# Moving VectorE's multiplications by g and its row scalings to other gaps of a fused attention and gated-FFN kernel

## The chip, the core and the metric

The kernel runs on one core of a Trainium2 chip. The metric is the device time of one execution in microseconds (us), as the median of several executions. The engines are named as in the profile: PE multiplies matrices (PEld is its weight load), DVE is the vector engine, ACT the scalar engine, POOL the general-purpose engine, SP the engine that only issues transfers here. Each engine runs its own instructions in the order in which the program lists them; engines wait for each other through semaphores.

## What is computed

Linear attention without a softmax, a normalisation of each head's row, and a gated feed-forward layer:

```python
kv  = einsum('bhsd,bhse->bhde', k, v)        # 8 batches, 8 heads, 576 tokens, head size 64
o   = einsum('bhsd,bhde->bhse', q, kv)
x   = o / sqrt(mean(o*o, -1) + 1e-6) * g_norm  # then (tokens 4608, columns 512)
ffn = (gelu(x @ w_gate) * (x @ w_val)) @ w_out
out = x + sigmoid(x @ w_res) * ffn
```

Inputs and outputs are float32; the kernel multiplies in float16 with float32 sums.

## The kernel before, in words

**Blocks.** The work is cut into nine blocks of 512 tokens: blocks 0 to 7 are the first 512 tokens of each batch, block 8 collects the 64 left over from each. The attention of a batch is computed one or two blocks ahead, in gaps of the feed-forward work. Per block a tile `t` (128 partitions x 4 rows x 512 columns, float16) holds x, a transposing DMA makes `xT` of it, and `th_all` and `res_all` (the `osb` of the profile) hold the gate and the result. `res_all` and `th_all` exist once.

**Making x.** `a_t` (L330, its instruction on L341) scales one quarter of the attention's result by the rows' inverse norms: it reads the product in PSUM (`op`) and the norms in SBUF (`ny`) and writes `t`. Its numbers 0 to 3 are the four quarters and 4 the left-over rows. `a_x` (L353, instruction on L355) multiplies one row of `t` by `g16`, the vector g, in place: both inputs and the output are float16 in SBUF. For block 1 the transposed copy gets its g elsewhere, and the four `a_x` of block 1 are for the residual sum alone. They are the lambdas `x` at L570.

**The gate and value products.** From block 2 on, the products with `w_gate` (suffix g) and `w_val` (suffix v) are made in groups of four column tiles by `gv_group` (L708), with seven half-size products instead of eight. A group follows a list of words written out by hand (`ORDERS`, L703). `1g` to `7g` and `1v` to `7v` are products of four matmuls each on PE (L737); `Eg`, `Ev` copy `A` to another PSUM bank and `dg`, `dv` copy `F` to SBUF, on ACT (L747, L751); `Fg`, `Fv`, `cg`, `cv` are additions on DVE (L758); `g11` and so on are gelus on ACT (L768); `h11`, `h12`, `h21` are multiplications on DVE and `h22` one on POOL (L774). The order of a group that is not its block's last:

```
1g 1v Eg 5g Ev 5v dg 6g dv 6v Fg 2g Fv 2v 7g g11 7v cg 3g cv 3v h11 g12 4g g21 h12 4v g22 h21 h22
```

Products 1, 6, 7 and 4 of a letter share the bank `A` of that letter, so 6 waits for the copy E, 7 waits until the addition F has read `A`, and 4 until the addition c has. The next group takes the banks in another order: its `E` is this group's `F`, its `F` this group's `E`. So its copy `Ev` waits for this group's `h12`, the last reader of that bank.

**Work in the gaps.** `at_word(blk, i, word, fs...)` (L1172) hangs further instructions behind a word of group i of block blk. They stand in the order of each engine at that place, so that a DVE instruction hung on `1v` comes ahead of `Fg` on DVE, one hung on `Fv` between `Fv` and `cg`, one hung on `cv` between `cv` and `h11`.

**The end of a block.** `out_by_products` (L497) makes the last product and the gate; `fin` (L529, instruction on L531) adds `t` to a half of `res_all` on POOL, and `store` (L533, issue on L536) sends two rows to HBM from SP's queue. For block 1 the flag `later` is set, and `fin`, `store` and block 1's `a_x` are hung on words of the first group of block 2 (L569 to L574). Block 2 has its first columns in another form and then two groups; blocks 3 to 6 (`whole`, L1175) have three groups each. `plan_attn_ahead` (L1179) hangs the scalings `a_t` of batch b in block b-1 (its m+1): numbers 0 and 1 at the end of the block before it, numbers 2 and 3 in group 0 and number 4 in group 1 (L1220 to L1233).

The two places that the change touches and what calls them:

Of the kernel before, what the change touches and what calls it, by code (L numbers as in the profile page):

```python
# [18 lines left out]
def kernel(  # L19
# [392 lines left out]
    def m_res(blk, j, bank):  # L412
        rps = pmoe.tile([P, C], FP32, name="rps", bank=bank)
        for cc in range(NP):
            nc.tensor.matmul(  # L415
                rps,
                lhsT=xT_t[blk][:, j, cc, :],
                rhs=wr16[:, cc, :],
                start=(cc == 0),
                stop=(cc == NP - 1),  # L420
            )

        th = th_all[:, j, :]
        nc.scalar.activation(out=th, in_=rps, func=AF.Tanh, scale=0.5)  # L424
        return th
# [33 lines left out]
    def a_of(blk, i, j):  # L459
        return hids[blk][:, (j - 1) * NFH : j * NFH, (i - 1) * PR : i * PR]  # L460
# [20 lines left out]
    def s_last(blk):  # L481
        sub(nc.vector, hid_sums[3], a_of(blk, 1, 2), hid_sums[1])

    def prod(ps, a, b, start, es=(0, 1)):

        for e in es:
            for f in range(NFH):
                nc.tensor.matmul(  # L488
                    ps[:, e - es[0], :],
                    lhsT=a[:, f, e * P : (e + 1) * P],  # L490
                    rhs=b[:, f, :],
                    start=(start and e == es[0] and f == 0),
                    stop=(f == NFH - 1),
                    skip_group_check=True,
                )

    def out_by_products(blk, later, banks, amid):  # L497
        w = {}
        s_ = hid_sums

        def aside(ahead_of):
            for f in amid.get(ahead_of, ()):
                f()

        def res(jj):
            for j in (2 * jj, 2 * jj + 1):
                m_res(blk, j, banks[j])

        def first_two():
            for n in ("D", "E", "F", "A"):  # L510
                w[n] = pmoe.tile([P, 2, CH], FP32, name="w" + n, bank=banks[n])
            w["d"] = attnp.tile([P, 2, CH], FP32, tag="sq", bufs=3, name="wd")
            s_last(blk)
            prod(w["A"], a_of(blk, 1, 1), b_of(1, 1), True)
            nc.scalar.copy(out=w["E"], in_=w["A"])
            aside("D")
            prod(w["D"], s_[0], wo_t[:, 0], True)
            nc.scalar.copy(out=w["d"], in_=w["D"])
            aside("gates")
            for j in range(NJ):  # L520
                m_sigmoid(j)

        def part(jj):
            return slice(None), slice(2 * jj[0], 2 * jj[0] + 2), slice(jj[1] * CH, (jj[1] + 1) * CH)

        def pf(jj, src, eng=nc.vector):
            eng.tensor_tensor(out=res_all[part(jj)], in0=th_all[part(jj)], in1=src, op=ALU.mult)  # L527

        def fin(jj):  # L529
            of = part(jj)  # L530
            nc.gpsimd.tensor_tensor(out=res_all[of], in0=res_all[of], in1=t_t[blk][of], op=ALU.add)  # L531

        def store(jj):  # L533
            dst = out[blk * S : blk * S + M0, :].rearrange("(p j) c -> p j c", j=NJ)
            js = slice(2 * jj, 2 * jj + 2)
            nc.sync.dma_start(out=dst[:, js, :], in_=res_all[:, js, :])  # L536

        def others():


            prod(w["A"], s_[1], wo_t[:, 1], False)
            aside("F")
            sub(nc.vector, w["F"], w["A"], w["d"], ALU.add)
            aside("00")
            prod(w["E"], a_of(blk, 1, 2), b_of(2, 1), False)
            pf((0, 0), w["E"])
            aside("22")
            prod(w["A"], s_[2], wo_t[:, 2], False)
            c22 = res_all[part((1, 1))]
            sub(nc.vector, c22, w["A"], w["d"], ALU.add)  # L550
            aside("01")
            prod(w["F"], s_[3], b_of(2, 2), False)
            pf((0, 1), w["F"])
            aside("11")
            prod(w["A"], a_of(blk, 2, 2), wo_t[:, 3], False)
            if whole(blk + 1):
                pf((1, 1), c22, nc.gpsimd)
                pf((1, 0), w["A"])
            else:
                pf((1, 1), c22)  # L560
                pf((1, 0), w["A"])
            if later:
                return
            for i in (1, 0):
                fin((i, i))
                fin((i, 1 - i))
                store(i)

        if later:  # L569
            x = [lambda j=j: a_x(blk, j) for j in range(NJ)]  # L570
            at_word(blk + 1, 0, "1v", *x[0:2], lambda: fin((0, 0)), lambda: fin((0, 1)), lambda: store(0))
            at_word(blk + 1, 0, "Fv", x[2])
            at_word(blk + 1, 0, "cv", x[3])
            at_word(blk + 1, 0, "h22", lambda: fin((1, 0)), lambda: fin((1, 1)), lambda: store(1))  # L574
        return [lambda: res(0), lambda: res(1), first_two, others]

# [244 lines left out]
    for which in "kv":  # L821
        if which == "k":
            t = hidp.tile([P, NF, NJ * P], FP16, tag="hid", name=which + "f").rearrange("p a b -> p (a b)")
        else:
            t = hid_s
# [8 lines left out]
    for which in "kv":  # L834
        t = hid_of[which]
# [336 lines left out]
    def at_word(blk, i, word, *fs):  # L1172
        amid_gv.setdefault((blk, i), {}).setdefault(word, []).extend(fs)

    def whole(blk):  # L1175

        return WHOLE <= blk < B - 1

    def plan_attn_ahead(b):  # L1179

        rem = pair(b) is not None
        m = b - 2
        assert rem == (m in GROUPS)
        act, pool = nc.scalar.copy, nc.gpsimd
        begin = [lambda: attn_begin(b), lambda: d_qT(b)]
        if rem:
            begin.append(lambda: d_rem_qT(b))
        if m in GROUPS:
            for i in range(2):
                half = lambda i=i: by_token(b, act, slice(2 * i, 2 * i + 2))  # L1190
                if whole(m):
                    at_word(m, i, "g11", half)
                else:
                    at(m, 2 + i, half)
            if whole(m):
                at_word(m, 1, "g11", *begin)
            else:
                at(m, 3, *begin)
            if b + 1 < B:
                at(m, 2 * GF, lambda: load_behind(b))  # L1200
            last = len(GROUPS[m]) - 1
        else:
            at(m, 8, lambda: by_token(b, act, slice(0, 2)))
            at(m, 9, lambda: by_token(b, act, slice(2, 4)), *begin)
            at(m, NF - 1, lambda: a_kv(b, act))
            at(m, NF, lambda: load_behind(b))
        if rem:
            own = 2 * pair(b) + 1 == b
            at_word(m, last, "5v" if own else "3v", lambda: a_rem_kv(b))
            at_word(m, last, "dv" if own else "g12", lambda: kv_out(b))  # L1210
            at_word(m, last, "h21", *[lambda: rem_mm(b)] * own, lambda: rem_out(b), lambda: a_sq(b, NJ))
        at(m, NF, lambda: a_o(b), *[lambda: a_red(b, NJ)] * rem, lambda: a_ss(b, 0), lambda: a_ss(b, 1))
        aside_out(m, "D", lambda: a_ss(b, 2), lambda: a_ss(b, 3))
        aside_out(m, "F", lambda: a_norm(b, 0, NJ + rem, pool))
        first = [lambda: new_block(b), lambda: a_t(b, 0), lambda: a_t(b, 1)]
        if whole(m + 1):
            aside_out(m, "11", *first)
        else:
            at(m, NF + 3, *first)
        if whole(m + 1):  # L1220
            t = [lambda j=j: a_t(b, j) for j in range(NJ + 1)]
            x = [lambda j=j: a_x(b, j) for j in range(NJ + 1)]
            for i, word, fs in (
                (0, "Fv", t[2:3]),
                (0, "cv", t[3:4]),
                (1, "1v", x[0:1]),
                (1, "Fv", t[4:5]),
                (1, "cv", x[1:2]),
                (2, "1v", [*x[2:4], lambda: d_xT(b, 0, NJ)]),
                (2, "Fv", [x[4], lambda: d_xT(b, NJ, NJ + 1)]),  # L1230
            ):
                at_word(m + 1, i, word, *fs)
            return  # L1233
        for j in range(2, NJ + rem):
            at(m + 1, j - 2, lambda j=j: a_t(b, j))
        for j in range(NJ):
            at(m + 1, 2 + j // 2, lambda j=j: a_x(b, j))
        at(m + 1, 3, lambda: d_xT(b, 0, NJ))
        if rem:
            at_word(m + 1, 0, "h21", lambda: a_x(b, NJ), lambda: d_xT(b, NJ, NJ + 1))  # L1240
# [13 lines left out]
    for blk in GROUPS:  # L1254
        t = token_sums(blk, nc.vector)
# [160 lines left out]
```

## Time and profile before

| what | value |
|---|---|
| median of 4 runs | 324.74 us (324.45 to 325.05) |
| the profiled execution | 324.51 us, span 322.7 us |
| granted PE clock, mean | 0.996 |
| busy share PE, DVE, ACT, POOL | 98%, 82%, 62%, 45% |
| `a_x` (L355), 36 of them | shortest 408 ns, median 418 ns, longest 1271 ns |
| `a_t` (L341), 32 of them | 680 to 693 ns |
| `fin` on POOL (L531), 28 of them | 1151 to 1167 ns |

The profiled execution's own time exceeds its span by 1.8 us, which lies before the first and after the last instruction. A row of the timeline gives the start in us from the span's start, the duration in us, engine, line, operation, out<-in and, in brackets, how long the engine stood idle before it and which event ended that. Matmuls overlap: a row of four starts 0.44 us after the row before it and is shown as 0.60 us long, and ends of matmuls are modelled. So PE can be shown as busy through a stretch in which it lost time, and what counts is the distance of the starts.

### The profile page before, as it was taken

How to read it: one execution, taken by the hardware profiler on the slowest of the kernel's cores; microseconds unless marked ns; L12 is line 12 of the kernel's file. 1: busy time of each engine (PE TensorE's matmuls, PEld its weight loads, DVE VectorE, ACT ScalarE, POOL GpSimd, SP SyncE). 2: the span in 40 equal slices, each digit the busy share in tenths (PEclk: the TensorE clock that was granted, in tenths of full speed). 3: DMA queues.
4: the chain of work that ended last, by engine and by line, in shares of the span. 5: the costliest groups of instructions: out<-in, count | busy, mean ns of one | idle time of the engine just before them, and what ended most of it. 6: DMA issues, size and time to landing. Idle time of an engine off the chain costs nothing.

```text
span 322.7 us, 7458 instructions
## 1 busy us (share of the span) xinstructions
PE 314.9 (98%) x2936; PEld 236.6 (73%) x2936; DVE 263.9 (82%) x482; ACT 201.4 (62%) x367; POOL 144.9 (45%) x212
## 2 busy tenths in 40 slices
PE   8999999999999999999999999999999999999993
PEld 3545755444857878887888688868887888788782
DVE  5788879799799887998799879998896777677754
ACT  3773675365737784878486848684766467636760
POOL 2792341573702779237833784117511342042232
PEclk9999999999999999999999999999999999999998
DMA  8999999798995599399938893710321030002004
GB/s 252 326 205 204 194 205 181 168 191 122 162 130 107 171 138 100 125 165 123 108 132 162 111 122 131 134 34 2 130 46 37 2 130 4 0 34 101 0 2 130
DMA packets 76693, 38.89 MB, mean 120 GB/s; under 512 B 42098, under 2 KB 74354, under 8 KB 76658
## 3 DMA queue, kind: packets, MB, share of 16 engines
q0 software_dynamic: 38752, 17.17, 42.2%
q1 hardware_dynamic: 37328, 20.71, 24.5%
q10 hardware_dynamic: 578, 0.52, 0.5%
q8 instruction: 23, 0.38, 0.5%
q14 instruction: 12, 0.10, 0.1%
HBM read 38.80 MB, written 9.44 MB: 149 GB/s over the span
## 4 chain that ended last, share of the span: by engine, by line
PE 96%; DVE 3%; issue 0%; DVEq 0%
PE Av L737 12%; PE Ag L737 12%; PE wA L488 11%; PE rps L415 10%; PE gps L395 6%; PE vps L395 6%; PE Fv L737 6%; PE Fg L737 6%; PE fps L432 3%; PE wE L488 3%; PE Eg L737 3%; PE Ev L737 3%; PE wF L488 3%; PE wD L488 3%; PE w L488 2%; PE idle L902 2%
## 5 line engine op out<-in xcount | busy, mean ns | idle before, releaser
L774 POOL TENSOR_TENSOR hid<-ge,c 128x512 f16<-128x512 f16 x21 | 24.4, 1163 | 68.8 <-ACT ge L768 68.8
L531 POOL TENSOR_TENSOR osb<-osb,t 128x512 f32<-128x512 f32 x28 | 31.5, 1158 | 36.1 <-DVE osb L527 25.1
L488 PEld LDWEIGHTS <-hid_s 128*128 128x128 f16 x384 | 37.6, 98 | 4.4
L737 PEld LDWEIGHTS <-wsv 128*128 128x128 f16 x336 | 32.8, 98 | 4.4
L737 PEld LDWEIGHTS <-wsg 128*128 128x128 f16 x336 | 32.8, 98 | 3.8
L415 PE MATMUL rps<-wr,xT 128*128 128x512 f16 x144 | 33.4, 380 | 0.0
L488 PEld LDWEIGHTS <-hid 128*128 128x128 f16 x288 | 28.2, 98 | 5.0
L747 ACT COPY Eg<-Ag 128x512 f32<-128x512 f32 x21 | 12.2, 582 | 25.9 <-PE Ag L737 25.9
L758 DVE TENSOR_TENSOR Fg<-Ag,d 128x512 f32<-128x512 f32 x21 | 14.7, 698 | 16.4 <-ACT d L751 11.1
L383 ACT ACTIVATE ge<-gps 128x512 f16<-128x512 f32 x24 | 14.1, 597 | 21.3 <-PE gps L395 21.1
L737 PEld LDWEIGHTS <-wg 128*128 128x128 f16 x252 | 24.4, 98 | 3.7 <-issue 0.4
L737 PEld LDWEIGHTS <-wv 128*128 128x128 f16 x252 | 24.6, 98 | 3.3 <-issue 0.2
L424 ACT ACTIVATE th<-rps 128x512 f32<-128x512 f32 x36 | 21.1, 595 | 8.1 <-PE rps L415 8.0
L737 PE MATMUL Ag<-ts,wsg 128*128 128x256 f16 x168 | 25.2, 273 | 0.0
L737 PE MATMUL Av<-ts,wsv 128*128 128x256 f16 x168 | 25.2, 272 | 0.0
L254 DVE TENSOR_REDUCE ss<-sq 128x8 f32<-128x512 f32 x32 | 20.1, 678 | 5.8 <-ACT sq L249 5.8
L415 PEld LDWEIGHTS <-xT 128*128 128x128 f16 x144 | 13.5, 98 | 14.2
L395 PE MATMUL gps<-xT,wg 128*128 128x512 f16 x88 | 22.6, 379 | 0.0
L395 PE MATMUL vps<-xT,wv 128*128 128x512 f16 x88 | 22.6, 379 | 0.0
L488 PE MATMUL wA<-wo_ts,hid_s 128*128 128x256 f16 x168 | 20.6, 273 | 0.0
L384 DVE TENSOR_TENSOR hid<-ge,vps 128x512 f16<-128x512 f16 x24 | 16.3, 685 | 4.8 <-PE vps L395 4.0
L429 ACT ACTIVATE th<-th 128x512 f32<-128x512 f32 x36 | 20.1, 642 | 0.0
(188 smaller groups left out, 765.6 us busy)
## 6 DMA issues: line engine op xcount, KB each, us to landing
out_dram<-osb SPq DMA_DIRECT2D x14, 512.0 KB, 2.6
qraw<-in_q_dram POOLq DMA_DIRECT2D x7, 512.0 KB, 7.0
k<-in_k_dram POOLq DMA_DIRECT2D x7, 512.0 KB, 10.4
v<-in_v_dram POOLq DMA_DIRECT2D x7, 512.0 KB, 11.3
wg<-in_moe_w_gate_dram POOLq DMA_DIRECT2D x2, 512.0 KB, 8.1
wv<-in_moe_w_val_dram POOLq DMA_DIRECT2D x2, 512.0 KB, 8.6
wo<-in_moe_w_out_dram POOLq DMA_DIRECT2D x2, 512.0 KB, 13.8
out_dram<-osb SPq DMA_DIRECT2D x4, 256.0 KB, 4.5
```

The source lines that it names most:

```text
L254: nc.vector.tensor_reduce(out=out_, in_=sqs.pop((b, i)), op=ALU.add, axis=mybir.AxisListType.X)
L383: nc.scalar.activation(out=ge, in_=gps, func=AF.Gelu)
L384: nc.vector.tensor_tensor(out=hids[blk][:, f, :], in0=ge, in1=vps, op=ALU.mult)
L395: nc.tensor.matmul(ps[:, j0 * P : j1 * P], lhsT=w[:, cc, :], rhs=xT_t[blk][:, j0:j1, cc, :], start=(cc == 0 and j0 == 0), stop=(cc == NP - ...
L415: nc.tensor.matmul(rps, lhsT=xT_t[blk][:, j, cc, :], rhs=wr16[:, cc, :], start=(cc == 0), stop=(cc == NP - 1),)
L424: nc.scalar.activation(out=th, in_=rps, func=AF.Tanh, scale=0.5)
L429: nc.scalar.activation(out=th, in_=th, func=AF.Copy, scale=0.5, bias=0.5)
L488: nc.tensor.matmul(ps[:, e - es[0], :], lhsT=a[:, f, e * P : (e + 1) * P], rhs=b[:, f, :], start=(start and e == es[0] and f == 0), stop=( ...
L531: nc.gpsimd.tensor_tensor(out=res_all[of], in0=res_all[of], in1=t_t[blk][of], op=ALU.add)
L737: nc.tensor.matmul(out_[:, r, :], lhsT=lhsT, rhs=rhs, start=(first and r == 0 and c == 0), stop=(c == 1), skip_group_check=True,)
L758: nc.vector.tensor_tensor(out=dst, in0=ps["A", u], in1=sb["d", u], op=ALU.add)
L774: eng.tensor_tensor(out=dst, in0=ge[q], in1=source(q, "v"), op=ALU.mult)
```

## The change

Two pieces of the order are moved. No instruction is added, removed or resized.

```diff
         if later:
             x = [lambda j=j: a_x(blk, j) for j in range(NJ)]
-            at_word(blk + 1, 0, "1v", *x[0:2], lambda: fin((0, 0)), lambda: fin((0, 1)), lambda: store(0))
+            at_word(blk + 1, 0, "1v", *x[0:2])
             at_word(blk + 1, 0, "Fv", x[2])
-            at_word(blk + 1, 0, "cv", x[3])
+            at_word(blk + 1, 0, "cv", x[3], lambda: fin((0, 0)), lambda: fin((0, 1)), lambda: store(0))
             at_word(blk + 1, 0, "h22", lambda: fin((1, 0)), lambda: fin((1, 1)), lambda: store(1))
...
             for i, word, fs in (
-                (0, "Fv", t[2:3]),
-                (0, "cv", t[3:4]),
+                (0, "1v", t[2:3]),
+                (0, "Fv", t[3:4]),
                 (1, "1v", x[0:1]),
                 (1, "Fv", t[4:5]),
                 (1, "cv", x[1:2]),
```

The first piece concerns block 1's rows, whose end is worked off in the first group of block 2. POOL's first two sums and SP's first store are listed after the fourth multiplication by g instead of after the second. The four multiplications keep their places on DVE.

The second piece concerns group 0 of blocks 3 to 6. Scaling 2 of the next batch moves from behind `Fv` to behind `1v`, ahead of `Fg` on DVE, and scaling 3 from behind `cv` to behind `Fv`, into the place that scaling 2 leaves.

## Prediction

> **What bounds the kernel now.** I read the clock of the core first (0.996, so nothing is lost to throttling), then the chain of waits.
>
> ```profile
> ## 4 chain that ended last, share of the span: by engine, by line
> PE 96%; DVE 3%; issue 0%; DVEq 0%
> ```
>
> The kernel is bound by PE: a change of other engines' order is worth what it takes off PE's own stalls, and nothing else. The list of PE's waits shows one in this part of the kernel, 0.2 us of `Ag` on DVE's `c`. That list misses small stalls, because matmuls overlap and a late one leaves no idle time in the records. The distance between the first matmul of one group and of the next does not miss them. The view by windows, for group 0 of block 2 and for group 1 of blocks 3, 4, 5 and 6 (columns: stretch, its length, then PE busy and the rest):
>
> ```profile
> 97.89:104.50 6.61, 6.43 (x57) 5.47 (x56) 6.46 (x13) 4.42 (x8) 2.27 (x2) 1.00 0.63 118
> 131.19:137.54 6.35, 6.35 (x59) 5.45 (x56) 5.93 (x12) 5.30 (x10) 1.16 (x1) 1.00 0.23 86
> 164.24:170.35 6.11, 6.11 (x58) 5.48 (x56) 5.97 (x12) 5.25 (x10) 1.16 (x1) 1.00 0.22 86
> 197.10:203.46 6.36, 6.36 (x59) 5.46 (x56) 5.94 (x12) 5.30 (x10) 1.16 (x1) 1.00 0.24 90
> 230.25:236.36 6.11, 6.11 (x58) 5.47 (x56) 5.97 (x12) 4.32 (x9) 1.16 (x1) 1.00 0.20 81
> ```
>
> The same fourteen products take 6.11 us in blocks 4 and 6 (14 x 0.437) and more elsewhere: 0.50 us too much in block 2, 0.24 in block 3, 0.25 in block 5. Group 0 of blocks 3 to 6 takes 6.16 each. These are the sums that can be had here: 0.50 + 0.24 + 0.25 + 4 x 0.05 = 1.19 us.
>
> **Block 2: a multiplication held by POOL.** The timeline around the stall:
>
> ```profile
> 100.27 2.27 POOL L531 TENSOR_TENSOR osb<-osb,t 128x512 f32<-128x512 f32 x2 [10.60 <-DVE t L355]
> ...
> 101.55 1.27 DVE L355 TENSOR_TENSOR t<-t,g 128x512 f16<-128x512 f16 x1
> ...
> 102.69 0.60 PE L737 MATMUL Fv<-xT,wsv 128*128 128x256 f16 x4
> 102.74 0.68 DVE L758 TENSOR_TENSOR c<-Ag,d 128x512 f32<-128x512 f32 x1
> ...
> 103.34 0.67 DVE L758 TENSOR_TENSOR c<-Av,d 128x512 f32<-128x512 f32 x1
> 103.47 0.60 PE L737 MATMUL Ag<-ts,wg 128*128 128x256 f16 x4 [0.18 <-DVE c L758]
> ...
> 103.94 0.41 DVE L355 TENSOR_TENSOR t<-t,g 128x512 f16<-128x512 f16 x1
> 104.07 0.60 PE L737 MATMUL Av<-ts,wv 128*128 128x256 f16 x4
> ```
>
> The third multiplication by g takes 1.27 us where the fourth takes 0.41. It starts inside POOL's two sums (100.27 to 102.54) and ends at 102.82, 0.28 after them: it was held until POOL was done. Everything behind it on DVE is late: `cg` starts at 102.74 and `cv` ends at 104.01. Product 4g is due 0.437 after 3v, at 103.13, and starts at 103.47; 4v is due at 103.57 and starts at 104.07, just behind `cv`.
>
> After the change POOL's sums wait for the fourth multiplication, so the third takes 0.41 and ends at 101.96. `cg` then waits for product 7g alone (101.38 + 0.60 = 101.98) and runs to about 102.70, `cv` to 103.30. Both are ahead of 103.13 and 103.57: 4g and 4v start on time, and the whole 0.50 goes.
>
> What is queued behind the sums: on POOL `h22` of this group, and the two sums of rows 3 and 4; on SP the first store, with the second behind it. The fourth multiplication ends near 103.65, the sums at 103.7 + 2 x 1.14 = 106.0, `h22` (105.30 now) at 107.15, the other two sums at 109.4. POOL's next piece, `h22` of the second group, starts at 110.07 now and could start some 0.5 earlier, at 109.6: still behind them. The stores go to HBM at 106.0 and 109.4 instead of 105.84 and 108.70, with 2.6 us to landing (the table of issues); `res_all` is written again by the gate of block 2, at 121.46. No other DVE multiplication by g lies between 103.7 and 109.4, so nothing new is held there. Cost of the move: nothing; if that cover were gone, up to 0.7 us of POOL's delay would show.
>
> **Blocks 3 to 6: the scalings.** DVE in block 3, before:
>
> ```profile
> 125.74 0.68 DVE L527 TENSOR_TENSOR osb<-th,wA 128x512 f32<-128x512 f32 x1
> 127.62 0.70 DVE L758 TENSOR_TENSOR Fg<-Ag,d 128x512 f32<-128x512 f32 x1 [1.20 <-ACT d L751]
> ...
> 128.82 0.68 DVE L341 TENSOR_TENSOR t<-op,ny 128x512 f16<-128x512 f32 x1
> ...
> 131.81 0.68 DVE L774 TENSOR_TENSOR hid<-ge,Fv 128x512 f16<-128x512 f16 x1
> ```
>
> Scaling 2 goes into the 1.20 us of idle time ahead of `Fg`: 126.34 to 127.02, 0.60 before `Fg` can start. Its inputs are ready: scalings 0 and 1 read the same norms at 124.54. Scaling 3 takes the place of scaling 2, so `Fg`, `Fv`, `cg`, `cv` keep their times to 130.70. Hence the 0.05 of group 0 (4v waits for `cv`) stays: nothing is had in group 0.
>
> Behind `cv` a scaling of 0.60 is gone, and `h11`, `h12`, `h21` come 0.60 earlier. `h12` ends at 131.90 instead of 132.49. ACT's copies `Eg` and `Ev` of group 1, blocks 3 and 4:
>
> ```profile
> 131.92 0.59 ACT L747 COPY Eg<-Ag 128x512 f32<-128x512 f32 x1
> 132.86 0.57 ACT L747 COPY Ev<-Av 128x512 f32<-128x512 f32 x1 [0.34 <-PE Fg L737]
> ...
> 164.98 0.59 ACT L747 COPY Eg<-Ag 128x512 f32<-128x512 f32 x1
> 165.63 0.57 ACT L747 COPY Ev<-Av 128x512 f32<-128x512 f32 x1
> ```
>
> `Ev` has to wait for `h12`. In block 4 `h12` ends at 165.54 and `Ev` starts at 165.63; in block 3 it ends at 132.49 and `Ev` starts at 132.86, 0.28 later than in block 4 against the same products. The releaser that the row names, product 5g, is none: block 4 doesn't wait for it (165.11 + 0.60 is after 165.63). Numbering ACT's records in the trace, `Ev` of block 3 is number 191 and that of block 5, as late, number 319: 128 apart. The table of queues has instruction loads of 0.10 MB in 12 packets, 8 KB each, which is 128 records of 64 bytes. So I read the 0.28 as the step to the next piece of ACT's program, which the sequencer can take only when the wait for `h12` is over. The step before, at number 63 (45.31), shows no delay: ACT was still working on the instruction ahead of it. The same should hold here when `h12` ends at 131.90: the wait is over when `Eg` starts (131.92), the step falls under `Eg`, and `Ev` starts at about 132.44, as 0.48 behind `Eg` in block 2 (105.20, 105.68). Then 6v is no longer late (0.11 now, 133.48), nor 7v behind it (0.09), nor 4v (0.04): 0.24 in block 3, 0.25 in block 5. Block 3 gives 0.05 back in group 2: block 4, on time in group 1, takes 20.59 from group 2 to the next block (170.35 to 190.94), block 3 20.54 (137.54 to 158.08), with 7v of group 2 0.50 and 0.46 behind 7g, because DVE's queue is no earlier.
>
> The Trainium skill speaks against this reading. Runtime: NRT & Kernel Launch, Instruction fetch mechanics, says that the sequencer fetches the next part of the program while it runs the present one, and that a crossing is mostly hidden. By the page the 0.28 has another cause and may stay, and the sum would be 0.50; by the rows it is 0.94.
>
> DVE is no earlier because the next multiplication by g, hung on 1v of group 1, is held as in block 2. Now it starts at 133.01 under POOL's `h22` (132.10 to 133.26) and ends at 133.55, 0.29 after it. Started at 132.41 it meets the same `h22` and ends at the same time. That cost I set at 0; its bounds are -0.14 us per block (not held at all, `Fg` earlier by what ACT allows) and +0.10 (held for its full 0.41 after POOL's end, less the slack of `Fg`).
>
> **The sum.** 0.50 + (0.24 - 0.05) + 0.25 = 0.94 us. Against the profiled execution: 324.51 - 0.94 = 323.57. The median of the four runs is 0.23 higher (324.74), and by it the sum is 323.80. I take 323.7.
>
> **The rivals.**
> 1. Only block 2's stall goes, because `Ev`'s 0.28 does not depend on when `h12` ends. For it: it is a reading by number, and the named releaser is another. Then -0.50: 324.0 to 324.24. Chance 0.20.
> 2. Block 2's stall stays, since another wait ends just as late (PE's 4v behind ACT or POOL). Against it: the second group of block 2 has the same words and `cv` 0.60 behind `cg`, without a stall. Then -0.44: 324.1 to 324.3. Chance 0.07.
> 3. Slower: scaling 2, now ahead of `Fg`, is held by POOL's four sums as the multiplication by g was (they run 125.81 to 130.30). It decides when the hold goes past 127.82, since `Fg` has 0.20 to spare before 7g. Held to the end of all four it ends at 130.58, 7g is 2.8 late, four times over: +11, less 0.94, about 335. Against it: the same operation at 128.82 takes 0.68 inside these sums. Chance 0.05, most of it for a shorter hold or another small delay there, 0.3 to 1 us per block.
> 4. The forecast: 0.68.
>
> **How the numbers follow.** About 0.2% (0.65 us) is what a measurement of this kernel can tell from no change: below 324.09 is faster. The forecast lies there but for a little scatter (0.64 of 0.68), rival 1 with a fifth of its chance (0.04), and rivals 1 and 2 otherwise within: faster 0.68, same 0.27, slower 0.05. The range takes in the forecast with its bounds (323.57 less 4 x 0.1) and rivals 1 and 2: 323.2 to 324.3.
>
> **What would show it.** Right: the third multiplication in block 2 at 0.41 and group 0 at 6.11; scaling 2 in front of `Fg` at 0.68; `Ev` of block 3's group 1 some 0.5 behind `Eg`, and groups 1 of blocks 3 and 5 at 6.11. Wrong: `Ev` still 0.9 behind `Eg` (rival 1), `cv` of block 2 still ending after 103.57 (rival 2), `Fg` of blocks 3 to 6 later than 2.6 us behind 1g (rival 3).

## The result and the profile after

| | before | changed |
|---|---|---|
| median, all runs | 324.57 us (70 runs) | 324.11 us (45 runs) |
| ratio, 95% interval | | 0.9983 (0.9977 to 0.9990) |
| the profiled execution, its span | 324.51, 322.7 us | 324.22, 322.4 us |
| from the first 1g of block 2 to the 1g of the last group of block 8 | 97.89 to 298.35: 200.46 us | 97.98 to 298.01: 200.03 us |

The changed kernel is faster by 0.17%, about 0.55 us by the ratio (its interval is 0.32 to 0.75 us) and 0.43 us by the two traces from block 2 on. The forecast was 0.94 us of gain (323.7), so about half of it came. The time lies inside the range of 323.2 to 324.3. The gain is a little below the 0.2% that the prediction took for the least that can be told from no change, but the interval of the ratio leaves out 1.

The last row of the table is the one that I use below. It leaves out the opening, which lies ahead of everything that the change touches and still differs from execution to execution: over the profiles of all the kernels in this study, block 2 starts at any time from 97.62 to 98.54.

The view by windows of the changed kernel, group 0 of block 2 and group 1 of blocks 3, 4 and 5:

```profile
97.98:104.60 6.62, 6.44 (x58) 5.46 (x56) 6.47 (x13) 4.43 (x8) 2.27 (x2) 1.00 0.63 118
131.29:137.40 6.11, 6.11 (x58) 5.49 (x56) 6.01 (x11) 5.17 (x10) 1.16 (x1) 1.00 0.21 84
164.15:170.26 6.11, 6.11 (x58) 5.49 (x56) 6.01 (x11) 5.17 (x10) 1.16 (x1) 1.00 0.22 86
197.01:203.12 6.11, 6.11 (x58) 5.47 (x56) 6.01 (x11) 5.17 (x10) 1.16 (x1) 1.00 0.22 87
```

Blocks 3 and 5 have lost their 0.24 and 0.25, as forecast. Block 2 has kept its 0.50. The timeline of the changed kernel there shows why:

```profile
98.86 1.43 DVE L355 TENSOR_TENSOR t<-t,g 128x512 f16<-128x512 f16 x4
...
100.36 2.27 POOL L531 TENSOR_TENSOR osb<-osb,t 128x512 f32<-128x512 f32 x2 [10.60 <-DVE t L355]
...
101.64 1.27 DVE L355 TENSOR_TENSOR t<-t,g 128x512 f16<-128x512 f16 x1
...
103.44 0.68 DVE L758 TENSOR_TENSOR c<-Av,d 128x512 f32<-128x512 f32 x1
103.57 0.60 PE L737 MATMUL Ag<-ts,wg 128*128 128x256 f16 x4 [0.18 <-DVE c L758]
104.04 0.41 DVE L355 TENSOR_TENSOR t<-t,g 128x512 f16<-128x512 f16 x1
```

POOL's sums start at 100.36, in the same place as before (100.27 there, in an execution that is 0.09 earlier throughout). They stand in the list behind the fourth multiplication by g, which begins at 104.04, and do not wait for it: what releases them is still the second one, the last of the four of the first row, which end at 100.29. The third is held as before and takes 1.27 us.

In block 3 the scalings stand where the prediction put them. The timeline of DVE in the changed kernel:

```profile
125.84 0.68 DVE L527 TENSOR_TENSOR osb<-th,wA 128x512 f32<-128x512 f32 x1
126.44 0.69 DVE L341 TENSOR_TENSOR t<-op,ny 128x512 f16<-128x512 f32 x1
127.72 0.70 DVE L758 TENSOR_TENSOR Fg<-Ag,d 128x512 f32<-128x512 f32 x1 [0.59 <-ACT d L751]
...
131.31 0.68 DVE L774 TENSOR_TENSOR hid<-ge,Fv 128x512 f16<-128x512 f16 x1
...
132.51 1.14 DVE L355 TENSOR_TENSOR t<-t,g 128x512 f16<-128x512 f16 x1
```

and of ACT, the two copies of group 1:

```profile
132.02 0.59 ACT L747 COPY Eg<-Ag 128x512 f32<-128x512 f32 x1
132.54 0.56 ACT L747 COPY Ev<-Av 128x512 f32<-128x512 f32 x1
```

`Fg` keeps 0.59 of its 1.20 us of idle time, so the scaling ahead of it costs nothing. `h12` (131.31) ends at 131.99, `Ev` follows `Eg` by 0.52 us instead of 0.94, and the multiplication by g that now begins at 132.51 takes 1.14 us: it ends at 133.65, 0.29 behind POOL's `h22` (132.20 to 133.36), as the prediction had it.

### The profile page after: what moved, and what is told of

Read it like the earlier page. It is cut to its first block, busy times and chain, and to the rows that moved or that the text cites. A ratio compares the mean times of both kernels' runs of the same rounds, so it can differ in the third digit from the quotient of the medians.

```text
span 322.4 us, 7458 instructions
## 1 busy us (share of the span) xinstructions
PE 314.4 (98%) x2936; PEld 236.8 (73%) x2936; DVE 266.6 (83%) x482; ACT 201.1 (62%) x367; POOL 145.1 (45%) x212
## 4 chain that ended last, share of the span: by engine, by line
PE 96%; DVE 3%; issue 0%; DVEq 0%
PE Ag L737 12%; PE Av L737 12%; PE wA L488 11%; PE rps L415 10%; PE gps L395 6%; PE vps L395 6%; PE Fv L737 6%; PE Fg L737 6%; PE fps L432 3%; PE wE L488 3%; PE wD L488 3%; PE Ev L737 3%; PE Eg L737 3%; PE wF L488 3%; PE w L488 2%; PE idle L902 2%
```

## Experiments

Eight kernels. The distance from block 2 to the last group, worked out as in the table above, and the ratios of the times:

| run | block 2 to last group | against before | ratio of times, 95% interval |
|---|---|---|---|
| before | 200.46 | | |
| changed | 200.03 | -0.43 | 0.9983 (0.9977 to 0.9990) |
| e1, first piece alone | 200.44 | -0.02 | 0.9999 (0.9986 to 1.0011) |
| e2, second piece alone | 200.02 | -0.44 | 0.9993 (0.9983 to 1.0004) |
| e3, sums that must wait | 199.96 | -0.50 | 0.9982 (0.9974 to 0.9991) |
| e4, e3 with the second piece | 199.53 | -0.93 | 0.9979 (0.9970 to 0.9987) |
| e5, before, one ACT record more | 200.01 | -0.45 | 0.9975 (0.9963 to 0.9987) |
| e6, before, seventeen more | 200.58 | +0.12 | 0.9998 (0.9985 to 1.0012) |
| e7, e4 with both scalings in the first gap | 199.36 | -1.10 | 0.9953 (0.9938 to 0.9967) |
| e8, changed, one ACT record more | 200.03 | -0.43 | one execution only |

Every interval holds the gain that the groups of its trace show. The intervals are wide, and where two kernels differ by a few tenths of a us the argument rests on the groups.

**e1 and e2: each piece alone.** The diffs are the first and the second half of the change.

> The first piece of the change alone. Theory 1 (a sum on POOL waits only for the rows that it reads, whatever else is listed ahead of it on another engine): nothing moves, POOL's sums start right behind the second multiplication by g, the third is held for 1.27 us, group 0 of block 2 takes 6.61 us, the time is that of before within 0.1 us. Rival (the place in the list counts): the third multiplication takes 0.41 us, group 0 takes 6.11 us, the time is 0.5 us shorter.

> The second piece of the change alone. Theory 1: the whole gain of the change is here, 0.43 us, with group 1 of blocks 3 and 5 at 6.11 to 6.15 us instead of 6.35 and Ev 0.5 us behind Eg. Rival (the two pieces share the gain): 0.2 us or less.

e1 is the kernel before: in the two traces every engine has the same instructions in the same order, and the times agree, with the sums at 100.23, the third multiplication at 1.27 us and group 0 of block 2 at 6.61 us. Theory 1 holds. A place in the list behind another engine's instruction made no wait here. The first two sums read rows 1 and 2, which the second multiplication finishes, and POOL has nothing else between the two places in the list. So the first piece changes nothing at all.

e2 has the whole gain by the trace: 0.44 us, `Ev` 0.52 us behind `Eg` and group 1 at 6.11 in all of blocks 3 to 6. Its ratio alone would not show it, since its interval includes 1.

**e3: sums that really wait.** On POOL the sums of rows 3 and 4 come first. They read what the third and the fourth multiplication write.

```diff
-            at_word(blk + 1, 0, "1v", *x[0:2], lambda: fin((0, 0)), lambda: fin((0, 1)), lambda: store(0))
+            at_word(blk + 1, 0, "1v", *x[0:2])
             at_word(blk + 1, 0, "Fv", x[2])
-            at_word(blk + 1, 0, "cv", x[3])
-            at_word(blk + 1, 0, "h22", lambda: fin((1, 0)), lambda: fin((1, 1)), lambda: store(1))
+            at_word(blk + 1, 0, "cv", x[3], lambda: fin((1, 0)), lambda: fin((1, 1)), lambda: store(1))
+            at_word(blk + 1, 0, "h22", lambda: fin((0, 0)), lambda: fin((0, 1)), lambda: store(0))
```

> The kernel before, with POOL's first two sums made those of rows 3 and 4, hung on cv, and those of rows 1 and 2 last. The sums that come first now read what the third and fourth multiplication by g write. Theory 1 (POOL's sums hold the third multiplication, and only a real dependence keeps them off): the third multiplication takes 0.41 us, cg starts about 0.65 us behind product 7g, group 0 of block 2 takes 6.11 us, the time falls by 0.5 us. Rival (PE's stall there has another cause, for instance ACT): the multiplication is short, group 0 stays above 6.4 us.

The timeline of e3, and its view by windows for group 0 of block 2:

```profile
101.28 0.42 DVE L355 TENSOR_TENSOR t<-t,g 128x512 f16<-128x512 f16 x1
...
102.36 0.68 DVE L758 TENSOR_TENSOR c<-Av,d 128x512 f32<-128x512 f32 x1
102.95 0.42 DVE L355 TENSOR_TENSOR t<-t,g 128x512 f16<-128x512 f16 x1
...
103.45 2.27 POOL L531 TENSOR_TENSOR osb<-osb,t 128x512 f32<-128x512 f32 x2 [14.05 <-DVE t L355]
...
105.68 1.17 POOL L774 TENSOR_TENSOR hid<-ge,c 128x512 f16<-128x512 f16 x1
105.74 3.68 SPq L536 DMA_DIRECT2D out_dram<-osb  x2
```

```profile
97.62:103.73 6.11, 6.11 (x57) 5.47 (x56) 5.90 (x13) 4.26 (x8) 0.28 (x1) 1.00 0.58 110
```

Now the sums start behind the fourth multiplication (103.45), the third takes 0.42 us, `cv` ends at 103.04 ahead of 4v (103.29), and group 0 of block 2 takes 6.11 us (97.62 to 103.73). The gain is 0.50, the term that the prediction had for block 2. Its list of what is queued behind the sums holds as well: `h22` of the group starts at 105.68, SP's stores from 105.74 on, and no group behind it is longer than before.

**e4: both at once.** e3 with the second piece of the change.

> The sums of rows 3 and 4 first, as in the run before this one, and the second piece of the change. If the two gains are independent: 0.50 + 0.43 = 0.93 us below the kernel before, 0.5 below the changed kernel. If the second eats into the first: 0.6 us or less below the kernel before.

The gains add: 0.93 us from block 2 on. This is the sum of the prediction, reached by a change that makes its first piece work. In this profile the opening is late (block 2 starts at 98.54, in e3 at 97.62), which is why its profiled time, 324.24 us, shows less of it than the groups do. Its ratio does not show the 0.93 by itself: the interval stands for 0.42 to 0.97 us.

**e5 and e6: where the step in ACT's program falls.** To the kernel before, copies of one number are added on ACT at the end of block 1, where ACT is idle. Each takes 173 to 188 ns there, and the scalings stay in their old places. A record is one entry of ACT in the trace, the sequencer's waits included, and the first has number 0.

```diff
+    mark = consts.tile([1, N], FP32, name="mark")   # N = 1 in e5, 17 in e6
+    aside_out(1, "11", *[lambda i=i: nc.scalar.copy(out=mark[:, i : i + 1], in_=eps_col[0:1]) for i in range(N)])
     out_at = {}
```

> The kernel before with one copy of a single number added on ACT, in ACT's idle time at the end of block 1; the scalings stay where they were. Theory 1 (Ev of group 1 is late in blocks 3 and 5 because it is the first record of a new piece of ACT's program, and the step is taken only when the record before it, the wait for h12, is over): with one more record the wait itself becomes the first record of the piece, the step falls under the wait, Ev starts 0.08 to 0.1 us behind h12's end as in block 4, group 1 of blocks 3 and 5 takes 6.11 us and the time falls by 0.4 us though h12 is as late as before. Rival (h12's lateness itself costs it): Ev 0.37 us behind h12, 6.35 us, no change of the time.

> The same with seventeen such copies. Theory 1: Ev of group 0 in blocks 3 and 5, number 174 before, becomes number 191, behind a wait for DVE: it starts about 0.28 us later against 1g (1.76 instead of 1.48), and group 0 of these blocks grows from 6.16 to about 6.3 to 6.45 us, while group 1 falls to 6.11: the time stays within 0.2 us of before. Rival: group 0 stays at 6.16 and group 1 at 6.35.

The timeline of DVE in e5, block 3:

```profile
132.19 0.68 DVE L774 TENSOR_TENSOR hid<-ge,Fv 128x512 f16<-128x512 f16 x1
```

and of ACT:

```profile
132.30 0.59 ACT L747 COPY Eg<-Ag 128x512 f32<-128x512 f32 x1
132.95 0.57 ACT L747 COPY Ev<-Av 128x512 f32<-128x512 f32 x1
```

`h12` ends at 132.87, 1.31 us behind 1g (131.56), as late as before the change. Record 191 is now the wait for `h12`, and `Ev` is record 192. `Ev` starts 0.08 behind `h12` instead of 0.37, and group 1 takes 6.11 us in blocks 3 and 5. So `h12`'s lateness by itself cost nothing. By the traces, one record more on ACT is worth as much as the whole change.

In e6 the step falls on group 0. The timeline of ACT in e6, block 3:

```profile
126.14 0.57 ACT L747 COPY Eg<-Ag 128x512 f32<-128x512 f32 x1 [4.12 <-PE Ag L737]
127.27 0.57 ACT L747 COPY Ev<-Av 128x512 f32<-128x512 f32 x1 [0.56 <-PE Fg L737]
```

and its view by windows, groups 0 and 1 of block 3, then of block 5:

```profile
125.50:131.94 6.44, 6.40 (x58) 5.45 (x56) 4.96 (x9) 4.53 (x8) 5.21 (x5) 1.00 0.35 109
131.94:138.05 6.11, 6.11 (x58) 5.48 (x56) 5.98 (x12) 5.26 (x10) 1.16 (x1) 1.00 0.17 67
...
191.49:197.93 6.44, 6.40 (x58) 5.45 (x56) 4.97 (x9) 4.53 (x8) 5.22 (x5) 1.00 0.30 105
197.93:204.04 6.11, 6.11 (x58) 5.49 (x56) 5.97 (x12) 5.25 (x10) 1.16 (x1) 1.00 0.18 69
```

`Ev` of group 0 starts 1.77 behind 1g, where before it was 1.48, and the 0.28 now sits there: 6.44 instead of 6.16 in blocks 3 and 5, not in 4 and 6 (6.16 and 6.16), while group 1 is free of it. The stall goes with the number of the record, from block to block and from group to group. The DMA packets in the traces fit a step between two pieces of ACT's program. Behind records 191 and 319, which are 128 apart, starts one load of instructions of 8 KB each: in the kernel before at 133.55 and 199.70 us (0.69 and 0.92 behind the records), in e6 at 128.21 and 193.93 (0.94 and 0.67), and none is left near the old places. In the changed kernel both loads are there too (133.22 and 198.78), without a stall: the step is still taken at the same records, and only its cost is gone. The load starts after the late `Ev` has started, so the 0.28 us is not a wait for that load. What the sequencer does in it is not recorded.

**e7: both scalings in the first gap.** On top of e4:

```diff
-                (0, "1v", t[2:3]),
-                (0, "Fv", t[3:4]),
+                (0, "1v", t[2:4]),
```

> As the run with the sums of rows 3 and 4 first and the scalings early, but both scalings in the gap behind 1v. Theory 1 (group 0 of blocks 3 to 6 takes 6.16 instead of 6.11 us because 4v waits for cv, and cv is late by the scaling ahead of cg): cg and cv come 0.5 us earlier, Fg some 0.06 us later, still in time for 7g, Fv about 0.03 late for 7v; group 0 takes 6.12 to 6.15 us and 0.1 us is gained over that run. Rival (Fg gets late for 7g): group 0 longer than 6.16, the time up to 0.5 us longer.

The timeline of DVE in e7, block 3:

```profile
125.74 1.28 DVE L341 TENSOR_TENSOR t<-op,ny 128x512 f16<-128x512 f32 x2
127.02 0.70 DVE L758 TENSOR_TENSOR Fg<-Ag,d 128x512 f32<-128x512 f32 x1
127.62 0.69 DVE L758 TENSOR_TENSOR Fv<-Av,d 128x512 f32<-128x512 f32 x1
128.56 0.69 DVE L758 TENSOR_TENSOR c<-Ag,d 128x512 f32<-128x512 f32 x1 [0.25 <-PE Ag L737]
```

Two scalings fill the gap exactly; `cg` now waits for its product and no longer for DVE. Group 0 of blocks 3 to 6 takes 6.11 to 6.13 instead of 6.16 us, 0.17 us in all by the distance from block 2. This version is faster than both kernels: its median of 6 runs is 323.32 us, 0.9953 of the kernel before, and its longest run, 323.53, is below the shortest of the changed kernel, 323.78.

**e8: the two ways of removing the stall together.** The changed kernel with one record more on ACT.

> The changed kernel with one copy of a single number added on ACT at the end of block 1. If the extra record and the early scalings take away the same stall, nothing is left to gain: group 1 of blocks 3 to 6 stays at 6.11 us and every other group as in the changed kernel (6.62 in block 2, 6.16 in group 0). If they are two gains that happened to have one size, some group gets another 0.2 us shorter.

Every group is as in the changed kernel (6.61 in block 2, 6.16 and 6.11 in blocks 3 to 6), 200.03 us. The record and the early scalings remove the same stall.

## Why the prediction was right, and where not

- **The time.** It lies in the range, but partly by luck. Of the forecast's two halves one came (0.44 of 0.94 us) and the other did not, and the range reached up to 324.3 to take in rivals 1 and 2, each of which leaves about one half of the sum.
- **What can be had.** Confirmed by e7: reading the distance of first matmuls gave 1.19 us of stalls from block 2 on, and removing them one by one has brought 1.10.
- **Block 2, the failed step.** The prediction said "After the change POOL's sums wait for the fourth multiplication". They don't. The term was 0.50 and measured 0 (e1: -0.02, no difference in the order of any engine). What followed from the sentence was sized rightly (e3: 0.50), and so was its cover; but the change does not do it. The place in the list was read as a wait across engines. In e1 it made none, and in e3, where the sums read what the fourth multiplication writes, they start 0.08 behind its end. That the sums run on POOL and the multiplications on DVE was known beforehand.
- **The rival for it** (rival 2) has the measured price, -0.44, by a wrong mechanism: it let another wait end as late, where the old one never went. The plain possibility that the first piece leaves every engine's order untouched was not among the rivals.
- **The scalings.** Right in each step. In front of `Fg` at no cost (126.44 to 127.13, `Fg` 2.60 us behind 1g, before 2.59); `cv` no earlier, so group 0 keeps 6.16; no hold by POOL's sums (0.69 us inside 125.91 to 130.41), so rival 3 is out.
- **`Ev` and the step.** Right: 0.24 + 0.25 less 0.05 given back in block 3, forecast 0.44, measured 0.43 (e2 0.44). From group 2 of block 3 to the next block the changed kernel takes 20.59 instead of 20.54. Rival 1 is out by e2, where the 0.28 goes when `h12` ends earlier; e5 and e6 bear out the reading by the number of the record, on which that rival cast doubt. One small slip: 0.48 behind `Eg` at 131.92 is 132.40, not 132.44. The measured distance is 0.52, which makes it 132.44, and the sum does not change.
- **The held multiplication** in group 1: set at 0, and it is 0; it starts 0.6 earlier and ends 0.29 behind `h22`, as before.
- **The step, by the page and by the runs.** The Trainium skill, Runtime: NRT & Kernel Launch, Instruction fetch mechanics, holds a crossing for mostly hidden. Here it is hidden where the engine still works on the record ahead of it (changed kernel, e5) and costs 0.28 us where the last record of a piece is a wait that ends late (before, e6). By the page the sum would have been 0.50, all of it in the place that brought nothing; the measurement decides.

## What to carry to other kernels

To move an instruction in a program that is listed for several engines, write down the order of each engine before and after: if none differs and no data dependence is new, expect nothing (200.44 against 200.46 us here). If another engine's piece has to come later, give it a dependence that makes it wait, here by working on the late rows first. On an engine that is the bound, compare the distances of equal groups of work rather than idle time, and look for the stall in the one group that is longer than its twins.

## What was not expected of the hardware

One instruction of 0.17 us on ACT, of no use to the result, makes this kernel 0.45 us faster by the trace, since it moves the step of ACT's program from `Ev` to the wait ahead of it; seventeen make it 0.12 us slower by the trace. A comparison of two versions of this kernel can thus contain 0.2 to 0.3 us per step (0.24 and 0.25 in e5, 0.28 in e6) that belong to the number of ACT's instructions and not to the edit.

The opening of the kernel varies by up to 0.9 us between profiled executions: between e3 and e4, whose instructions are the same up to block 2, the difference is 0.74 us at 12 us and 0.92 at block 2. This is as large as the effects studied. It is a likely reason for the wide intervals of the ratios, which no run tests, and the reason why the groups are compared in the traces.
